# Attention scores in a one-core attention and feed-forward kernel: from stacked operand tiles to pairs of matmuls in the two row halves of TensorE

## The chip, the cores and the metric

One core of one Trainium2 chip runs the whole program. The metric is the device time of one execution in microseconds (us); the median of three executions of the kernel before is 939.8 us. A difference of about 0.2% (some 2 us) is what such a measurement can tell from no change.

## What is computed

Thresholded attention over 8 batches, 8 heads, 576 positions and head dimension 64, then a feed-forward block (FFN) on the result. Everything is float32:

```
scores = scale * q @ k.T
thresh = max(scores, -1) - tau
scores = where(scores >= thresh, scores, -1e9)
attn   = softmax(scores)
x      = attn @ v                        # heads side by side: (8, 576, 512)
xk     = mu_k * x + (1 - mu_k) * x_prev  # x_prev: x one position earlier
xr     = mu_r * x + (1 - mu_r) * x_prev
out    = sigmoid(xr @ w_r) * (relu(xk @ w_k)**2 @ w_v)
```

The weights are 512x1024, 1024x512 and 512x512.

## The kernel before

**Work and order.** The program is recorded first: `add` notes each step with its engine, what it reads and writes, and a planner's cost, and `plan.follow(PLACES)` then puts all steps in the order of a table of numbers (lines 20 to 120). Each engine executes its steps in that order, and so does the one queue that issues DMAs (SP). Nothing is reordered at run time; a step that is not ready holds up what stands behind it on its engine.

**Jobs and units.** Two heads of a batch make a job. A batch has four jobs; in batch 0 each is cut in two halves. A job has units: four of kind P (128 queries of each head against 576 keys) and one of kind T (the last 64 queries of both heads together). There are 128 P units and 32 T units. Per unit: `scores` on TensorE into the PSUM tiles `s` (one per head, two in all); on VectorE the row maximum (line 660); on ScalarE the threshold (668) and the exponential (676); on VectorE the mask with the sum (684), which is the last reader of `s`; then GpSimd's scaling (713).

**Split operands.** The matmul type is fp32r, which keeps fewer bits than float32, so `operands` (479 to 570) splits the scaled q and k of a job into a high part (ScalarE, 521) and the remainder (GpSimd, 531), both in the tile `hl`, and a product is hi·hi + hi·lo + lo·hi. The host lays out q and k "woven": the rows of the two heads alternate. Six DMAs a job (545, 557, 563) pick each head's rows from `hl` and build two stacked tiles: `st1` has q's high and low parts on 128 rows with the high part of k twice; `st2` has the low part of k on the even rows and zeros on the odd ones (set once, 477). Two products of 128 rows then give all three terms. Per P unit and head: two products of two matmuls of 288 columns, four steps a unit at lines 613 to 628, the matmul in line 620.

**Other score paths.** The first four jobs (`plain`) use unsplit float32: a matmul of 64 rows for each head, head 0 in the upper and head 1 in the lower row half of the array (line 602; each matmul is two passes in the trace). The T units take three products of 128 rows straight from `hl` (line 592). Both stay as they are.

**Probabilities to the second product.** In batches 0 and 1 TensorE transposes the probabilities (738) and ScalarE evicts them (754). From batch 2 on a job is "moved": VectorE turns 32x32 blocks into the tile `pt` (774, 787; two units of a group fill one `pt`, of which there is one), a DMA writes it to DRAM (`far`, 798), and a second reads it back into `pm` in the order wanted (803). `attend` (line 930) multiplies by v, 64 columns of the array for each head, side by side.

**FFN.** `ffn_chunk` has the products with w_k (1089), w_r (1131) and w_v (1153), all of 128 rows in fp32r. They stand between the score steps on TensorE once batch 0 has its scores, and alone at the end. `FILL` steps (1245) are transposes of the identity that nothing reads.

Of the kernel before, what the change touches and what calls it, by code (L numbers as in the profile page):

```python
# [8 lines left out]
F32 = mybir.dt.float32  # L9
# [7 lines left out]
KEEP = ('st2', 's', 'w', 'pm', 'pl')  # L17
# [3 lines left out]
FILL = 11  # L21
PLACES = (
    "!$(%*0!%!.!,!0!B!#!!!&!/!)#i!*!f##!>#<#B#e$[!+!H!]!a!u!}#X#h!-!O!`$G$J$k%.%[!2#7#;#c#f$($+$F#O$h(+(5(G(l)I)Q!X#.$I(U",
    "(Z(f):)J#`&V(P)C)G)M)t*,!m#p&%&b&h&q&{)s!A$U)y*)*2*7*?*H#:#v)X)0)o*$*F*O#1$2*9*>*C*G*M*W!S!z*B*N*V*[*c*x!d#H*`*i*p*v",
    "+&+,&B*e*o+%+-+6+y,_#P+]+n,C,D,I,S-z)S+$+F+x+|,$-l/&%O&Z+9+<+N+V+s,1$#,:,s-K-_-e.%.,%I-s/A/7/F/M/R/^#I-=/m/p/s/t/{0;",
    "!(!<#?!1!3!6!7!:!4!9!8!=!@!C!E!D!M!V!I!T!L!W!?!J!P!Q!U!F!K!N!R![!^!b!_!h!q!c!g!l!t#!#%#*#-#6#G!;!s#~!Z!i!o!n!r!e!j!k",
    "!p!y!{!~#4#)#F#W#a#8#E!x#&#,#/#5#+#3#2#9#>#A#D#C#S#g#N#[#R#]#l#s#u#z#|$*!5#@$z#=#J#Q#L#T#K#U#V#Y#_#b#d#{#m$/$,$H$!$4",
    "#^#o#w#x#}#j#t#q#y$%$&$-$)$3$@$7$D$6$A$K$M$O$S$X%z!G!v&?!|#(#M$1#$#n#0#Z$.$$$0$:$9$<$5$=$;$?$C$E$L$P$]$c$g$t$V$^$B$N",
    "$R$T$Y$Q$W$Z$_$e$j$o$r$y%6%!%)$}%3%|&$&)&7&:&C$8$`%L&J(R&*&H&](=(I(_)r*-*8(j(s)L)i)w)z)|*!*6*<*@*D*J+3+Z+d+p+q+u+{,&",
    ",.,/,M,]-u.2.8+>+E+J+P+S+_+b+k,4,i-8-^,{-(-W-b-d-g-w-{.4.U/./3*U*]*b+.+5*Q*Y*h+2+@-X/?/C/L/Q/X070<0O0b1X0J0U0n0r0v11",  # L30
    "151;1B1U#r$>&}$p$w$~%#$u%1%9%D%>$d$i$m$s%$${%(%,%0%8%B%V%M%A%J%P$a$b$v$x$f$l$n$q$|%%%&%*%5%:%?%G%H%R%^%r%T%Y%4%7%+%/",
    "%;%C%F%K%2%<%=%E%W%_%c%g%q&F&,&9%v%x&j&l&r&v&w()(#%-%Z(i%h%u%~&&%t&;&#&+&/%N%Q%S%X%`%b%e%p&3&A&X&z(!&O&`(&%U%]%n%o%a",
    "%d%f%i%s%{%}&(&.&2&5&<&@&M&L&R&S&d%w%y&-&1&!&0&4&=&8&D&>&G&Q&U&i&a(*(4(/(J&|(1(Q(T(W(`(d(r(q&6&^)P&f&x&p(2&n(,(B(<(F",
    "&E&I&K&N&[&W&_&e(Y(^(g)8)3(m).)&&c&g&P&T&k&s&t&y&Y&m&o&u(((-(7(0(?(O(:(@(E(N&~($(3(6(.(>(8(A(;(C(D(L(X(a(k(c(w)+(~)/",
    "(t(x)<)Y)c(9(e+`(o(|)%)((z)>)B)1)7(H(K(M(S(](V(b(h)))9)f)l*#)h)~)x([(p(n(u(v({(})#(y)!)$)*)5)=)E)A)Z)_)N)U)`)j)2)4),",
    ")-)?)O)D)T)6)H)@)K)[)b)}*&*(*5*.*1*;*L*{+0+;/H*r+/,A,J,O,l-I.c/@/j/r/}0]0g0,0^0w1`2P2Z2]2t2y3!3,383=3A3E3]2e2g2x2|3$",
    "3)3M3e3i3q3u3x1~2+20282:2H2M2N2S2W2[2a1y1|2T2V2X2_2d2m3%3+31342232353D3Z3@3Q3U3Y3z464044494B4G4V4d4w5S5Y4-4>4J4R4Z4m",
    "4s4{5!58)F*f-O*t+4+?+D*}+O+U+=+c)R)V)W)])g)d)k*j*n+(+G+f+L+A+R+K)q)u)^)a){*+*%*/)e)m)n)v*4*=*a*A*w*|*I*R*g*k***E*3*:",
    "*S*X*Z*_*K*^*T*d*l*y+W+M+z,!+X+i+^+l,=,n,P*m*s*q*u*~+*+++1*z+!+#+)+r+v,)+},N,V,*,0,W,[+:+B+7+8+H+Q+T+[+C+I+a+g+o+t,,",
    "+w,7,;,3,8,<,Q,a,}+Y,+.s,@-&,H-<,F-J-6-B-F+e+h+j+m+~,(,-,?,B,f,x-E-3,o,z,y,#,%,5,9,2,6,L,R,>,E,G,K,Z,`,u,j-%-.-5-N-$",  # L40
    "-),T,U,X,^,Y,c,d,g,b,e,h,k,q,t,|-1---4-?-S-V-f.6.G.E,r,w,m,p-!-+-,-0,v,~-#-*-:->-C-R-]-i-k-t-q.*-/-2-9-;-7-D-@-G-A-L",
    "-H-Q-Z-`-h-n-|./...L-v.-.W.f-T.@0%.C.R._.{.w/$.[.P.k-M-P-U-Y-a-c-j.#.&.F.T.g.j.M.n.S-[-m-o-r-p-}-y.!-x.$-~.(.5.7.B.>",
    ".h.p.O.a.q.}.).+.1.3.0.;.9.=.:.?.<.A.J.N.o.Z.x/1/;/I/%/+/h0!/y.H.I.D.K.Q.X.Y.^.V.`.].b.i.t.v.|.~/5/0/d/(/9.d.e.m.r.l",
    ".u.z/!.y/)/#/-/>/E/J/O/b/q/T/]/W/Z/u01/*/a2z/g/n0)090P0c0L0T0X/4/6/8/=/N/D/S/Y/o040@0V0H0?0D0A/G/K/,///P/U/V/[/2/:/<",
# [234 lines left out]
def tile_threshold_attention_then_rwkv_ffn(  # L279
# [1039 lines left out]
```

## Time and profile before

| | |
|---|---|
| median of 3 runs | 939.8 us (939.23 to 940.68) |
| profiled execution | 939.09 us, of which the trace spans 937.2 us |
| TensorE matmuls (PE) | busy 902.6 us, 96% of the span, 5881 instructions |
| VectorE (DVE) | 695.9 us, 74% |
| GpSimd (POOL) | 673.0 us, 72% |
| ScalarE (ACT) | 634.7 us, 68% |
| DMA | 226.59 MB, 69.2% of 16 engines' span |
| granted TensorE clock | 0.998 of 2.4 GHz |

Busy time counts a matmul from its start to its modelled end. Matmuls overlap in the pipeline, so the duration of one is more than the distance from its start to the next one's start. PEld is the load of the stationary operand, which runs beside matmuls. A wait is the idle time of an engine just before an instruction, put down to what ended it.

### The profile page before, as it was taken

What the parts mean: (1) busy time and instruction counts of PE and PEld (TensorE: products, weight loads), DVE (VectorE), ACT (ScalarE), POOL (GpSimd) and SP (SyncE); (2) the same over time, 40 slices, a digit from 0 to 9 for tenths busy, and PEclk for the clock granted to TensorE, in tenths of its full rate; (3) what the DMA queues carried; (4) which work ended last, traced back from release to release, by engine and by line L of the source; (5) the groups of instructions that cost most, each with busy time, mean ns of one, the idle gap of its engine ahead of it and who ended that gap; (6) DMA issues with size and microseconds to landing.
All of it is one profiled execution on the core that took longest, in us unless ns stands there. A gap on an engine that the chain in (4) does not pass through costs nothing.

```text
span 937.2 us, 17207 instructions
## 1 busy us (share of the span) xinstructions
PE 902.6 (96%) x5881; PEld 739.3 (79%) x5881; DVE 695.9 (74%) x1503; ACT 634.7 (68%) x1284; POOL 673.0 (72%) x822
## 2 busy tenths in 40 slices
PE   5888999999999999999999999999999999999998
PEld 3465787788888788888887888888888888879986
DVE  4889998898878887888789978788788887810030
ACT  3799999977676767575766575768476766545532
POOL 2688898877778768686787587788678677746531
PEclk9999999999999999999999999999999999999999
DMA  8756333558898988998788878989888887750001
GB/s 316 258 174 203 106 104 115 161 183 305 295 312 307 330 303 316 315 311 301 273 286 299 299 264 314 312 299 315 279 302 313 302 306 266 259 176 23 23 23 23
DMA packets 102327, 226.59 MB, mean 242 GB/s; under 512 B 19296, under 2 KB 32608, under 8 KB 96096
## 3 DMA queue, kind: packets, MB, share of 16 engines
q1 hardware_dynamic: 102240, 225.49, 69.2%
q8 instruction: 47, 0.77, 0.3%
q14 instruction: 40, 0.33, 0.1%
HBM read 108.27 MB, written 73.14 MB: 194 GB/s over the span
## 4 chain that ended last, share of the span: by engine, by line
PE 69%; DVE 10%; ACT 9%; DMA 7%; issue 2%; SPq 1%; POOL 1%; ACTq 0%; DVEq 0%; POOLq 0%
PE w L1153 19%; PE w L1089 16%; PE w L930 12%; PE s L620 10%; PE w L1131 8%; ACT p L676 3%; DVE p L684 3%; DMA st<-hl 2%; DVE pt L774 2%; PE s L592 2%; DMA far<-pt 2%; ACT pm L754 2%; DVE sm L660 2%; PE w L738 1%; PE s L602 1%
## 5 line engine op out<-in xcount | busy, mean ns | idle before, releaser
L684 DVE SCALAR_TENSOR_TENSOR p<-s,sm,p 128x576 f32<-128x576 f32 x288 | 231.8, 811 | 50.8 <-ACT sm L668 24.6
L676 ACT ACTIVATE p<-s,sm 128x576 f32<-128x576 f32 x288 | 209.2, 734 | 84.4 <-DVE sm L660 57.4
L660 DVE TENSOR_REDUCE sm<-s 128x1 f32<-128x576 f32 x288 | 212.9, 750 | 62.1 <-PE s L620 41.6
L713 POOL TENSOR_SCALAR p<-p,sm 128x576 f32<-128x576 f32 x288 | 213.0, 749 | 43.2 <-DVE sm L704 39.8
L1089 PE MATMUL w<-xk,wk 128*128 128x256 f32 x1728 | 229.4, 281 | 0.1
L1153 PE MATMUL w<-wv,k 128*128 128x512 f32 x864 | 220.4, 395 | 0.0
L1089 PEld LDWEIGHTS w<-xk,wk 128*128 128x128 f32 x1728 | 217.0, 188 | 4.1 <-issue 1.6
L1153 PEld LDWEIGHTS w<-wv,k 128*128 128x128 f32 x864 | 156.8, 188 | 30.6 <-issue 1.2
L930 PE MATMUL w<-pm,v 128*64 128x256 f32 (+1 forms) x1280 | 165.4, 410 | 0.8 <-DVE xT L457 0.4
L930 PEld LDWEIGHTS w<-pm,v 128*64 128x64 f32 x1280 | 88.7, 137 | 66.2 <-issue 5.3
L668 ACT ACTIVATE sm<-sm,small 128x1 f32<-128x1 f32 x288 | 81.0, 289 | 68.8 <-DVE sm L660 68.2
L1112 POOL TENSOR_TENSOR k<-r,k 128x512 fp32r<-128x512 f32 x72 | 92.6, 1293 | 48.6 <-ACT k L1102 45.7
L774 DVE STREAM_TRANSPOSE pt<-p 128x1024 f32<-128x1024 f32 x96 | 115.9, 1217 | 5.1 <-DMA end<-pt 1.8
L620 PE MATMUL s<-st 128*128 128x288 f32 x480 | 108.6, 310 | 11.1 <-DVE p L684 10.2
L1131 PE MATMUL w<-wr,xk 128*128 128x512 f32 x432 | 112.6, 395 | 0.0
L531 POOL TENSOR_TENSOR hl<-raw,hl 128x640 fp32r<-128x640 f32 (+1 forms) x64 | 97.9, 1535 | 13.5 <-ACT hl L521 8.2
L696 POOL TENSOR_SCALAR sm<-sm 128x2 f32<-128x2 f32 (+1 forms) x160 | 30.7, 192 | 102.2 <-DVE p L684 84.8
L620 PEld LDWEIGHTS s<-st 128*128 128x128 f32 x480 | 78.7, 188 | 32.0 <-DVE p L684 20.3
L620 PE MATMUL s<-st,st 128*128 128x288 f32 x480 | 101.7, 297 | 0.2 <-DMA st<-hl 0.2
L1131 PEld LDWEIGHTS w<-wr,xk 128*128 128x128 f32 x432 | 77.6, 188 | 15.1 <-issue 0.5
L1097 ACT ACTIVATE r<-w 128x512 f32<-128x512 f32 x72 | 42.4, 594 | 61.5 <-PE w L1089 46.1
L620 PEld LDWEIGHTS s<-st,st 128*128 128x128 f32 x480 | 77.2, 188 | 2.7 <-DMA st<-hl 0.4
(71 smaller groups left out, 1026.3 us busy)
## 6 DMA issues: line engine op xcount, KB each, us to landing
far<-pt SPq DMA_DIRECT2D x48, 1152.0 KB, 5.1
pm<-far SPq DMA_DIRECT2D x48, 1152.0 KB, 6.2
st<-hl SPq DMA_DIRECT2D x64, 288.0 KB, 4.1
raw<-in_qk SPq DMA_DIRECT2D x28, 640.0 KB, 5.0
st<-hl SPq DMA_DIRECT2D x56, 256.0 KB, 3.9
v<-in_v SPq DMA_DIRECT2D x36, 320.0 KB, 3.9
st<-hl SPq DMA_DIRECT2D x64, 144.0 KB, 3.6
out<-sg SPq DMA_DIRECT2D x32, 256.0 KB, 3.8
```

The costliest lines, as they stand in the source:

```text
L531: lambda cs=cs: G.tensor_tensor(hl.get()[:, 1, cs], raw.get()[:, cs], hl.get()[:, 0, cs].bitcast(F32), op=ALU.subtract),
L620: PE.matmul(ss[y].get()[:, z, 0:HS], l.get()[:, c * P : (c + 1) * P], r[:, z * HS : (z + 1) * HS], start=(j == 0), stop=(j == 1),)
L660: lambda sv=sv, col=col: V.tensor_reduce(col(0), sv(), axis=AX.XY, op=ALU.max, negate=True),
L676: lambda sv=sv, pv=pv, col=col: A.activation(pv(), sv(), AF.Exp, bias=col(0)),
L684: lambda sv=sv, pv=pv, col=col: V.scalar_tensor_tensor(pv(), sv(), col(1), pv(), op0=ALU.is_ge, op1=ALU.mult, accum_out=col(2)),
L713: lambda y=y, o=y * S if unit["kind"] == "P" else 0: G.tensor_scalar(p.get()[:, o : o + S], p.get()[:, o : o + S], sm.get()[:, 3, y : y + ...
L774: V.transpose(o, x)
L930: PE.matmul(o[g].get()[hs, 0 : n[g]], vt.get()[:, c, hs], pt, start=(c == 0), stop=(c == 4))
L1089: PE.matmul(h.get()[:, f], l, r, start=(ct == 0 and i == 0), stop=(ct == NCT - 1 and i == 2))
L1112: lambda r=r, js=js: G.tensor_tensor(k2.get()[:, 1, js], r.get().rearrange("p (a b) -> p a b", a=2), k2.get()[:, 0, js].bitcast(F32), op=A ...
L1131: PE.matmul(z.get(), l, r, start=(ct == 0 and i == 0), stop=(ct == NCT - 1 and i == 2))
L1153: PE.matmul(vps.get(), l, r, start=(ft == 0 and i == 0), stop=(ft == NFT - 1 and i == 2))
```

## The change

- `st1`, `st2`, their six DMAs a job, the zeroing and the host's woven layout go. `hl` gets a second buffer.
- A P unit's scores become one step of twelve matmuls: for each of the three products and each half of the keys, head 0 in rows 0 to 63 and head 1 in rows 64 to 127 of the array, straight from `hl`. The step writes both `s` tiles.
- `pt` holds one unit in place of two, with two buffers, and each half goes to DRAM by a DMA of its own.
- The buffers `r` go from two to three, FILL from 11 to 17, and the table of places is a new one.

```diff
-FILL = 11
+FILL = 17
 PLACES = (
...
-    KTURN, KMOVE, RB, DMOVE, TB, FB = 0, 8, 2, 0.35, 1, 8
+    KTURN, KMOVE, RB, DMOVE, TB, FB = 0, 8, 3, 0.35, 2, 8
...
-        hl = job["hl"] = sbuf("hl", [P, 2, WM], FR)
+        hl = job["hl"] = sbuf("hl", [P, 2, WM], FR, 2)
...
-        job["st"] = [(sbuf("st1", [P, SM + S], FR, 3), sbuf("st2", [P, S], FR, 2)) for _ in range(2)]
...
-        for y in range(2):
-            st1, st2 = job["st"][y]
-            for j in range(2):
-
-                def mm(j=j, l=st1, y=y, st1=st1, st2=st2):
                     for z in range(2):
-                        r = st2.get() if j else st1.get()[:, nq - qt : nq - qt + S]
...
-                add("PE", 0.264, mm, reads=[st1, st2] if j else [st1], writes=[ss[y]], key=key + 0.5 * y - 1000, lat=0.44)
...
+        def mm():
+            qs = slice(qt + c * P, qt + (c + 1) * P)
+            for j, (l, r) in enumerate(prods):
+                for z in range(2):
+                    for h in range(2):
+                        hr = slice(h * D, (h + 1) * D)
+                        PE.matmul(
+                            ss[h].get()[:, z, 0:HS],
+                            hl.get()[hr, l, qs],
+                            hl.get()[hr, r, keys(h, z)],
+                            start=(j == 0),
+                            stop=(j == 2),
+                        )
+
+        add("PE", 0.95, mm, reads=[(hl, "hi"), (hl, ("lo", 0)), (hl, ("lo", 1))], writes=list(ss.values()), key=key - 1000, lat=1.15)
...
-                job["turned"][g] = sbuf("pt", [P, NQ, 2, BW], F32, TB)
+                job["turned"][g] = plan.buf(dram, "far", [P, NQ, 2, BW], F32, FB)
+            far, tt = job["turned"][g], sbuf("pt", [P, NQ, BW], F32, TB)
...
+            def away():
+                SY.dma_start(far.get()[:, :, t], tt.get())
+
+            add("DMA", DMOVE, away, reads=[tt], writes=[(far, t)], key=n - KMOVE, kb=576)
```

In the changed file line 577 is the new score matmul, 560 the T units', 883 the product with v, 1042, 1084 and 1106 the FFN's, 617 and 641 the row maximum and the mask, 751 and 757 the two DMAs of a moved group.

**TensorE, around a product with v.** Before (kernel lines as above; x2, x3, x10 count equal instructions in a row):

```order
L1089 MATMUL w_2_145<-xk_1_3105,wk20_0_529 128x256 x3
L620 MATMUL s_0_96<-st1_2_3092 128x288 x2
L1089 MATMUL w_2_145<-xk_1_3105,wk30_0_382 128x256 x3
L1089 MATMUL w_1_138<-xk_1_3105,wk21_0_1062 128x256 x3
L1089 MATMUL w_1_138<-xk_1_3105,wk31_0_788 128x256 x3
L620 MATMUL s_0_96<-st2_0_68,st1_2_3092 128x288 x2
L620 MATMUL s_1_98<-st2_1_70,st1_1_3173 128x288 x2
L1089 MATMUL w_1_138<-xk_1_3105,wk01_0_996 128x256 x3
L930 MATMUL w_0_119<-pm_0_160,v_0_3255 64x320 x10
L930 MATMUL w_2_145<-pm_1_277,v_0_3255 64x256 x10
L620 MATMUL s_0_96<-st1_0_3341 128x288 x2
L592 MATMUL s_1_98<-hl_0_3292 128x288 x6
```

Now (line 577's two rows alternate six times in each of the blocks):

```order
L577 MATMUL s_1_92<-hl_1_3338 128x288
L577 MATMUL s_0_90<-hl_1_3338 128x288
...
L1106 MATMUL w_3_170<-wv30_0_1921,k2_0_3629 128x512 x3
L1106 MATMUL w_2_162<-wv20_0_1544,k2_0_3629 128x512 x3
L1106 MATMUL w_2_162<-wv30_0_1921,k2_0_3629 128x512 x3
...
L577 MATMUL s_1_92<-hl_1_3338 128x288
L577 MATMUL s_0_90<-hl_1_3338 128x288
...
L883 MATMUL w_0_150<-pm_0_160,v_0_3675 64x320 x10
L883 MATMUL w_1_154<-pm_1_249,v_0_3675 64x256 x10
L577 MATMUL s_0_90<-hl_0_3750 128x288
L577 MATMUL s_1_92<-hl_0_3750 128x288
```

Before, score steps of 128 rows stand among FFN steps of 128 rows, two matmuls at a time; now each unit is one block of twelve matmuls of 64 rows, and some blocks stand right beside a product with v. In the whole order the array goes 99 times from one of its divisions (full, row halves, column halves) to another before, and 297 times now. There are 120 blocks at line 577; of their 240 edges 46 are shared with a product with v.

**VectorE, two P units in a row** (`sm` and `p` are of the unit, `s_0` and `s_1` of the head). Before:

```order
L684 SCALAR_TENSOR_TENSOR p_2_4794,sm_2_4770<-s_1_98,sm_2_4770,p_2_4794 128x576
L660 TENSOR_REDUCE sm_2_4770<-s_0_96 128x1
L660 TENSOR_REDUCE sm_1_4721<-s_1_98 128x1
L684 SCALAR_TENSOR_TENSOR p_2_4794,sm_2_4770<-s_0_96,sm_2_4770,p_2_4794 128x576
L704 RECIPROCAL sm_0_4711<-sm_0_4711 128x1
L684 SCALAR_TENSOR_TENSOR p_0_4729,sm_1_4721<-s_1_98,sm_1_4721,p_0_4729 128x576
```

Now:

```order
L617 TENSOR_REDUCE sm_1_4546<-s_1_92 128x1
L744 STREAM_TRANSPOSE pt_0_4553<-p_2_4443 128x4x32
L617 TENSOR_REDUCE sm_1_4546<-s_0_90 128x1
L641 SCALAR_TENSOR_TENSOR p_1_4559,sm_1_4546<-s_1_92,sm_1_4546,p_1_4559 128x576
L731 STREAM_TRANSPOSE pt_1_4573<-p_0_4512 128x2x4x128
```

Before, the next unit's first maximum could stand ahead of this unit's last mask; that is so between P units in 8 of 95 places, and in none now, since the block needs both `s` tiles free.

**SP, one job's DMAs.** Before:

```order
L545 DMA st1_1_3631<-hl_0_3621 128x1x512
L563 DMA st2_1_70<-hl_0_3621 64x576
L545 DMA st1_2_3748<-hl_0_3621 128x1x512
L557 DMA st1_2_3748<-hl_0_3621 128x1x576
L563 DMA st2_0_68<-hl_0_3621 64x576
L492 DMA raw_0_3782<-in_qk 128x1280
```

Now:

```order
L479 DMA raw_0_4480<-in_qk 128x1280
L751 DMA far_6_4504<-pt_0_4463 512x1x288
L751 DMA far_6_4504<-pt_1_4509 512x1x288
```

The 192 DMAs into `st1` and `st2` are gone, and 96 writes to `far` stand where 48 stood; the queue issues 470 DMAs in place of 614.

## Rows read from the trace of the kernel before

**Rows 1.** The page, part 1: busy time and share of the span.

```profile
PE 902.6 (96%) x5881; PEld 739.3 (79%) x5881; DVE 695.9 (74%) x1503; ACT 634.7 (68%) x1284; POOL 673.0 (72%) x822
```

**Rows 2.** Windows (from:to, length, busy of each engine with its count).

```profile
core 0: us, PE busy (x) PEld busy (x) DVE busy (x) ACT busy (x) POOL busy (x), PEclk, DMA share, GB/s
20.00:120.00 100.00, 87.69 (x572) 61.58 (x570) 88.39 (x192) 89.16 (x200) 81.82 (x107) 0.98 0.54 187
200.00:800.00 600.00, 595.46 (x3924) 495.77 (x3923) 494.64 (x1054) 399.12 (x787) 450.37 (x546) 1.00 0.86 299
```

**Rows 3.** The page, part 4: the chain that ended last, by engine.

```profile
PE 69%; DVE 10%; ACT 9%; DMA 7%; issue 2%; SPq 1%; POOL 1%; ACTq 0%; DVEq 0%; POOLq 0%
```

**Rows 4.** Waits of PE: for what, total us, times, longest.

```profile
PE s L620 <- DVE p L684: 10.2, 15, 1.8
PE s L602 <- ACT raw L500: 7.1, 1, 7.1
...
PE w L1245 <- ACT pm L754: 3.0, 3, 1.8
PE s L592 <- DVE p L684: 1.3, 1, 1.3
...
PE s L620 <- DMA st<-hl: 0.4, 2, 0.2
```

**Rows 5.** Timeline of PE near 403 us: start, length, instructions and their count.

```profile
403.30 0.43 PE L620 MATMUL s<-st,st 128*128 128x288 f32 x2
403.56 0.42 PE L620 MATMUL s<-st 128*128 128x288 f32 x2
403.83 0.43 PE L620 MATMUL s<-st,st 128*128 128x288 f32 x2
404.09 3.36 PE L1089 MATMUL w<-xk,wk 128*128 128x256 f32 x27
```

**Rows 6.** Lines by form: count, busy us, mean ns of one.

```profile
L620 PE MATMUL s<-st,st 128*128 128x288 f32 x480 | 101.7, 297 | 0.2 <-DMA st<-hl 0.2
L1153 PE MATMUL w<-wv,k 128*128 128x512 f32 x864 | 220.4, 395 | 0.0
L1089 PE MATMUL w<-xk,wk 128*128 128x256 f32 x1728 | 229.4, 281 | 0.1
L684 DVE SCALAR_TENSOR_TENSOR p<-s,sm,p 128x576 f32<-128x576 f32 x288 | 231.8, 811 | 50.8 <-ACT sm L668 24.6 <-ACT p L676 24.1 <-PE w L738 0.2
```

**Rows 7.** Line 602, row halves: duration ns min/median/max of each kind.

```profile
L602 PEld LDWEIGHTS s<-xk x32: 182/186/187, 31.5 to 47.0; 64*128 64x128 f32 x32
L602 PE MATMUL s<-xk x32: 402/403/507, 31.5 to 47.3; 64*128 64x288 f32 x32
```

**Rows 8.** Timeline of PE, 30.5 to 33.2 us: one P unit of line 602.

```profile
31.28 0.33 PE L738 MATMUL w<-ident,p 128*128 128x128 f32 x1
31.54 1.24 PE L602 MATMUL s<-xk 64*128 64x288 f32 x8
32.97 0.44 PE L738 MATMUL w<-ident,p 128*128 128x128 f32 x2 [0.19 <-POOL p L713]
```

**Rows 9.** Timeline of PEld, 31.53 to 31.66 us: the loads under way then.

```profile
31.54 0.30 PEld L602 LDWEIGHTS s<-xk 64*128 64x128 f32 x4
```

**Rows 10.** Timeline of PE, 386 to 395 us: a product with v between matmuls of 128 rows.

```profile
385.66 1.32 PE L1153 MATMUL w<-wv,k 128*128 128x512 f32 x5
386.91 5.07 PE L930 MATMUL w<-pm,v 128*64 128x320 f32 x40
391.91 0.52 PE L620 MATMUL s<-st 128*128 128x288 f32 x2
392.27 0.42 PE L620 MATMUL s<-st,st 128*128 128x288 f32 x2
```

**Rows 11.** Line 620's records up to 120 us (columns as in rows 2, PE and PEld alone).

```profile
0.00:120.00 120.00, 18.30 (x94) 13.58 (x94) 0.99 0.58 207
```

**Rows 12.** The chain in order of time: DMAs into the stacked tiles before 100 us.

```profile
69.71 3.77 DMA st<-hl
...
82.45 5.23 DMA st<-hl
```

**Rows 13.** DMA issues: count, KB each, median us to landing.

```profile
far<-pt SPq DMA_DIRECT2D x48, 1152.0 KB, 5.1
...
st<-hl SPq DMA_DIRECT2D x64, 288.0 KB, 4.1
```

More of the change, by code (lines that the diff above doesn't have):

```diff
@@ L578, in keys @@
         def keys(y, z):
-            k0 = nq - qt + (ST if unit["kind"] == "P" and y == 0 else 0)
+            k0 = nq + (ST if unit["kind"] == "T" or y == 0 else 0)
             return slice(k0 + z * HS, k0 + (z + 1) * HS)
-        if unit["kind"] == "T" and not job["plain"]:
-            hl = job["hl"]
-            prods = [(0, 0), (0, 1), (1, 0)]
-            for j, (v_, r) in enumerate(prods):
-                def mm(j=j, v_=v_, r=r):
-                    k = hl.get()[:, r, nq : nq + S + ST]
-                    for z in range(2):
-                        x = k[:, ST + z * HS : ST + (z + 1) * HS]
-                        PE.matmul(ss[1].get()[:, z, 0:HS], hl.get()[:, v_, 0:P], x, start=(j == 0), stop=(j == 2))
-                add("PE", 0.264, mm, reads=[(hl, ("lo", 0) if v_ else "hi"), (hl, ("lo", 1) if r else "hi")], writes=[ss[1]], key=key - 1000, lat=0.47)
-            return
         if job["plain"]:
@@ L612, in scores, with mm @@
             return
-        for y in range(2):
-            st1, st2 = job["st"][y]
-            for j in range(2):
-                def mm(j=j, l=st1, y=y, st1=st1, st2=st2):
+        hl = job["hl"]
+        prods = [(0, 0), (0, 1), (1, 0)]
+        if unit["kind"] == "T":
+            for j, (l, r) in enumerate(prods):
+                def mm(j=j, l=l, r=r):
                     for z in range(2):
-                        r = st2.get() if j else st1.get()[:, nq - qt : nq - qt + S]
                         PE.matmul(
-                            ss[y].get()[:, z, 0:HS],
-                            l.get()[:, c * P : (c + 1) * P],
-                            r[:, z * HS : (z + 1) * HS],
+                            ss[1].get()[:, z, 0:HS],
+                            hl.get()[:, l, 0:P],
+                            hl.get()[:, r, keys(1, z)],
                             start=(j == 0),
-                            stop=(j == 1),
+                            stop=(j == 2),
                         )
-                add("PE", 0.264, mm, reads=[st1, st2] if j else [st1], writes=[ss[y]], key=key + 0.5 * y - 1000, lat=0.44)
+                add("PE", 0.264, mm, reads=[(hl, ("lo", 0) if l else "hi"), (hl, ("lo", 1) if r else "hi")], writes=[ss[1]], key=key - 1000, lat=0.47)
+            return
+        def mm():
+            qs = slice(qt + c * P, qt + (c + 1) * P)
+            for j, (l, r) in enumerate(prods):
+                for z in range(2):
[6 more added lines that the diff above has]
+                            start=(j == 0),
+                            stop=(j == 2),
+                        )
+        add("PE", 0.95, mm, reads=[(hl, "hi"), (hl, ("lo", 0)), (hl, ("lo", 1))], writes=list(ss.values()), key=key - 1000, lat=1.15)
     def softmax(unit):
@@ L806, in back @@
                     )
-                add("DMA", DMOVE, away, reads=[tt], writes=[far], key=n - KMOVE, kb=1152)
                 add("DMA", DQ, back, reads=[far], writes=[(pm, "moved")], key=n - KMOVE, kb=1152)
```

244 lines of the change are left out of this document (95 added, 149 removed).

## The prediction

> **What bounds the kernel.** I read the busy times first, then the same by window, then the chain of waits and the waits themselves. TensorE is busy 96% of the span, VectorE 74% [rows 1]. By window there are two regimes [rows 2]: from 200 to 800 us TensorE is busy 595.5 of 600 us, VectorE 494.6; from 20 to 120 us TensorE is busy 87.7 of 100 us, with VectorE and ScalarE at 88 and 89. TensorE is 69% of the chain that ended last [rows 3]. It waited 11.5 us for masks to free the `s` tiles (10.2 + 1.3) and 0.4 us for the stacked tiles' DMAs [rows 4]. So after about 120 us a microsecond of TensorE's own time is a microsecond of the result, and the DMAs that go are hidden almost wholly. The question is what the scores cost TensorE in either form.
>
> **What goes.** 120 P units times 8 matmuls at line 620. Their distance from start to start is the cost, not their duration: six take 403.30 to 404.09, 0.132 us each [rows 5]. 960 x 0.132 = 126.7 us. A duration minus that distance, 297 - 132, is about 163 ns of pipeline that overlaps with the next one. By the same subtraction a matmul of line 1153 costs 395 - 163 = 232 ns [rows 6].
>
> **What comes.** 120 blocks of 12 matmuls of 64 rows. Whether two of them run side by side is read from line 602, which has this form in plain float32. Eight of its passes take 1.24 us [rows 8]. One lasts 402 ns, and 507 at most [rows 7]: the first ones carry 0.105 us in which they wait for their own weights. 1.24 - 0.163 - 0.105 = 0.97 us for eight passes, each of which streams 402 - 163 = 240 ns. One after the other they would need 1.9 us, so they go in four pairs, 0.243 us a pair. The weight loads go side by side too: four loads of 186 ns are done within 0.30 us [rows 7, 9]. So a block has six slots.
>
> A slot in fp32r is not in the trace. A float32 pass streams 288 columns in 240 ns, an fp32r matmul in 132. Bounds: 0.1215 us, half of line 602's pair, and 0.264, two matmuls of line 620 one after the other. I take 0.132, the nearest row: the same type and columns, and a pair reads the same 128 rows. 720 x 0.132 = 95.0 us (87.5 at the lower bound). The slots save 31.7 us.
>
> **What a change of the array's division costs.** Every block is cut off from its neighbours, which use 128 rows. The trace shows this price at the product with v [rows 10]. In front: five matmuls of 0.232 us should take 1.16 us from 385.66, but the product begins after 1.25, so 0.09 us are lost. Then comes the load that nothing hides, 0.105 us for 128 columns [rows 7] (half of that for the product's 64). Into a block: 0.195 us. Line 602 agrees: the transposition ahead of it starts at 31.28 and the first pass 0.26 us later, where two transpositions are 0.11 apart (0.44 - 0.33) and 0.05 is its own load [rows 8]. Behind: the product's 40 passes are ten pairs of 320 and ten of 256 columns; at 0.243 us per 288 columns they need 4.85 us, 0.05 more for the first load, and took 5.00 (386.91 to 391.91), so 0.10 us are lost. The next two matmuls then need 0.36 us in place of 0.264: 0.095 for the first load. Out of a block: 0.195 us, if row halves leave as column halves do.
>
> A block by itself costs 6 x 0.132 + 0.39 = 1.18 us, where the eight matmuls cost 1.06. Of the 240 edges 46 are shared with a product with v, which pays such edges already; a shared one saves one way out and one way in less what the common edge costs, about 0.195 us. In all 120 x 0.39 - 46 x 0.195 = 37.8 us. TensorE has 37.8 - 31.7 = 6.1 us more to do. Line 620 has 94 records before 120 us, 12 units [rows 11]; there TensorE has idle time [rows 2], and their part, 12 x 0.12 = 1.5 us, costs nothing. That leaves +4.6 us.
>
> The Trainium skill (TensorEngine Tiling (Array Packing), Key Properties) says that changing the tiling mode drains TensorE. The trace agrees: it is the 0.09 to 0.10 us above. The same page (Theoretical Speedup) promises up to 2x where the contraction has at most 64 rows and gives the change of mode no price; by that alone the sum would be -31.7 us, and the rows on the product with v speak against it.
>
> **Waits.** The twelve matmuls write both `s` tiles, so a block stands until this unit's second mask is done, where a head's own step needed its own mask alone. Behind it on TensorE stand FFN matmuls that were ready; VectorE's next maximum waits for the block. Where TensorE already waits (15 and 1 times [rows 4]), the wait can grow by a mask, 0.81 us [rows 6], some 13 us in all. That is the upper bound. Below: these 11.5 us can vanish, because TensorE, with more to do, comes later to each block; and two DMAs into stacked tiles on the early chain, 3.8 and 5.2 us [rows 12], go with the tiles. Between -20 and +13 I take 0: VectorE keeps a sixth of its time free, and the order of before already lets the next unit's first maximum pass the last mask in only 8 of 95 places.
>
> **The rest at nothing.** 192 DMAs fewer into the stacked tiles and 48 more, smaller ones to `far` [rows 13]: TensorE waited 0.4 us for the first kind; the half that is late (the second) is now half as large, and SP has fewer issues in front of every later one. If that cover failed, `pm` would be late and `attend` would stand. Six FILL steps are 18 transposes in the first units, where TensorE waits on ScalarE anyway [rows 4]; if not, 18 x 0.11 = 2 us [rows 8]. Two memsets of VectorE, ahead of the first scores, go. The third `r` buffer frees ScalarE earlier, which is not the bound.
>
> **Sum.** The profiled execution took 939.1 us (the median is 939.8). 939.1 + 4.6 = 943.7; I say 944 us, slower by half a per cent.
>
> **Rivals.**
> 1. *Cheap slots (faster).* A pair that costs half of line 602's, 0.1215 us, takes off 720 x 0.0105 = 7.6 us: 936. It turns the forecast to faster below 0.124 us a slot (720 x 0.0083 = 6 us). Waits for masks that vanish beside it would lead down to 928. For: line 602's pairs take 0.243 us where each pass streams 0.240, so pairing itself costs next to nothing. Against: every fp32r matmul of the trace needs more than half of what a float32 pass of its columns needs, 132 against 120 ns here, and a pair feeds as many rows.
> 2. *The joint wait (clearly slower).* Every block that is tied to the second mask makes a wait grow: 943.7 + 13 = 957. For: the block has no slack of half a unit. Against: see above.
> 3. *The halves don't run side by side in fp32r.* If a load of 0.105 us and a stream of 0.132 follow each other in each half, a slot takes 0.237: 720 x 0.105 = +76, 1020 us; with matmuls one after the other 0.264, 1039. Against: line 602, loads and all. The Trainium skill (TensorE: Matmul & The Clock Gate, Part 3) has a load overlap with running matmuls only where the row group differs, which would give this rival; the trace differs, since line 620 loads all 128 rows beside every matmul at 0.132 us.
> 4. *Edges without a price.* If the way in and out hid behind queued work, TensorE would have 31.7 us less: 907 us. Against: the product with v pays at both ends.
>
> **Chances.** The sum, 944 (its own range 939 to 952): 0.48, of which 0.34 slower by over 0.2% and 0.14 within it. Rival 1: 0.30 (0.27 faster, 0.03 the same). Rival 2: 0.12. Rival 3: 0.04. Rival 4: 0.06. So faster by over 0.2% (about what a measurement of this kernel can tell from no change) 0.33, the same 0.17, slower 0.50. The range for 8 in 10 is 928 to 960: it takes in rivals 1 and 2 and leaves out 3 and 4 and a little of each of the others.
>
> **What would show it.** At line 577 two matmuls start together and twelve take 0.8 us from the first to the last pair, at 0.132 a pair. TensorE loses 0.09 us in front of each block and 0.10 behind it, and the first matmuls on either side last 0.1 us longer than the others. FFN distances stay at 0.118 and 0.232. Waits of line 577 for the mask (641) stay near 11 us; at 25, rival 2 is right. Wrong is the whole if block and edges together take under 1.0 us (faster) or over 1.4.

## The result and the profile after

The changed kernel takes 947.97 us (five executions, 946.17 to 951.89), the kernel before beside it 939.8. The ratio is 1.0090, 95% interval 1.0062 to 1.0118. A second set (e14, six executions) gave 948.98 us and 1.0093 [1.0063, 1.0123]. So it is slower by 0.9%, some 8.5 us; the forecast was 944 us, 928 to 960. The profiled execution took 947.9 us.

The page, part 1, and the chain that ended last, by engine (before: [rows 1, 3]):

```profile
PE 910.9 (96%) x6379; PEld 716.1 (76%) x6379; DVE 697.8 (74%) x1501; ACT 631.2 (67%) x1284; POOL 672.3 (71%) x822
...
PE 86%; DVE 6%; ACT 4%; issue 1%; DMA 1%; POOL 1%; SPq 0%; ACTq 0%; DVEq 0%; POOLq 0%
```

Windows, as in [rows 2]:

```profile
core 0: us, PE busy (x) PEld busy (x) DVE busy (x) ACT busy (x) POOL busy (x), PEclk, DMA share, GB/s
20.00:120.00 100.00, 88.89 (x636) 61.82 (x635) 83.71 (x182) 85.77 (x196) 77.45 (x104) 0.98 0.38 130
200.00:800.00 600.00, 599.53 (x4308) 474.00 (x4305) 498.90 (x1062) 400.65 (x798) 454.06 (x551) 1.00 0.74 246
```

TensorE leaves 0.5 of 600 us unused, where it left 4.5. The DMA share of the middle falls from 0.86 to 0.74, and the DMAs drop out of the chain (1% where they were 7%). The stacked tiles were really a load; it was one that TensorE hardly felt.

A block of twelve matmuls between FFN matmuls, in the timeline of PE (compare [rows 5]):

```profile
403.39 2.99 PE L1042 MATMUL w<-xk,wk 128*128 128x256 f32 x24
406.31 1.06 PE L577 MATMUL s<-hl 64*128 64x288 f32 x12
407.31 3.97 PE L1042 MATMUL w<-xk,wk 128*128 128x256 f32 x31
```

The starts of the single matmuls in this stretch (the same trace, one by one): last FFN matmul 406.106; first pair at 406.315 and .318, the next ones at 406.552, .686, .815, .947 and 407.080; next FFN matmuls 407.305, 407.526, 407.646. Normal distances are 0.118 for the FFN and 0.132 for a pair. So 0.209 - 0.118 = 0.09 us are lost in front; the second pair comes 0.237 after the first, 0.105 too late; the pairs are 0.13 apart; 0.225 - 0.132 = 0.09 us are lost behind; and the second FFN matmul comes 0.221 after the first, 0.10 too late. Block and edges together are 1.185 us in the median of the blocks that stand among FFN matmuls.

Lines by form (compare [rows 6]):

```profile
L1042 PE MATMUL w<-xk,wk 128*128 128x256 f32 x1728 | 223.7, 284 | 0.0
L1106 PE MATMUL w<-wv,k 128*128 128x512 f32 x864 | 215.2, 399 | 0.0
L577 PE MATMUL s<-hl 64*128 64x288 f32 x1440 | 133.6, 310 | 8.5 <-DVE p L641 8.2
```

The FFN's matmuls last 3 to 4 ns longer in the mean (281 and 395 before), which is about what 0.1 us at each edge makes, spread over all of them. Waits of PE (compare [rows 4]):

```profile
PE s L577 <- DVE p L641: 8.2, 14, 1.4
PE s L542 <- DVE p L641: 7.6, 4, 2.7
PE s L542 <- ACT raw L487: 6.9, 1, 6.9
```

The blocks wait 8.2 us for masks, where line 620 waited 10.2. The `s` tiles as a whole cost as much as before: with the T units (0.5 now, 1.3 before) and the unsplit jobs (line 542, 7.6 now; before, the row below, which [rows 4] does not have) 16.3 us now and 15.6 before.

```profile
PE s L602 <- DVE p L684: 4.1, 3, 2.7
```

The waits for stacked tiles are gone.

What the joint step does shows at 158.7 us (timeline of PE, idle time before in brackets):

```profile
158.72 0.39 PE L577 MATMUL s<-hl 64*128 64x288 f32 x1 [0.76 <-DVE p L641]
159.53 1.06 PE L577 MATMUL s<-hl 64*128 64x288 f32 x11 [0.41 <-DVE p L641]
```

One matmul starts when the first head's mask is done, and the other eleven stand 0.81 us for the second head's mask, because the heads alternate in the block. Eight of the first 24 blocks (those of batches 0 and 1, up to about 195 us) show such a gap, 0.44 to 1.47 us; of the 96 later ones three, 0.46 to 0.62 us, between 518 and 537 us.

Last, the granted clock. TensorE ran at 0.5 of it (1.2 GHz) in two stretches of some 3.4 us, which the kernel before does not have there. The first, beside the same time in e13 (an experiment below that differs in the form of the first 24 blocks), by windows of PE:

```profile
core 0: us, PE busy (x), PEclk, DMA share, GB/s
92.00:94.00 2.00, 0.58 (x5) 1.00 0.04 15
94.00:96.00 2.00, 1.57 (x14) 1.00 0.00 0
96.00:98.00 2.00, 2.00 (x10) 0.56 0.00 0
98.00:100.00 2.00, 2.00 (x12) 0.59 0.00 0
```

and in e13:

```profile
92.00:94.00 2.00, 0.62 (x6) 1.00 0.03 8
94.00:96.00 2.00, 1.84 (x13) 1.00 0.00 0
96.00:98.00 2.00, 2.00 (x18) 1.00 0.00 0
98.00:100.00 2.00, 1.97 (x16) 1.00 0.27 64
```

Both waited some 1.4 us for a mask; only the changed kernel falls to half clock behind it. The block in the changed kernel also stands a second time (timeline of PE, the changed kernel's two rows and then e13's):

```profile
94.01 0.40 PE L577 MATMUL s<-hl 64*128 64x288 f32 x1 [1.43 <-DVE p L641]
94.83 1.06 PE L577 MATMUL s<-hl 64*128 64x288 f32 x11 [0.42 <-DVE p L641]
...
93.72 1.60 PE L592 MATMUL s<-hl 128*128 128x288 f32 x9 [1.38 <-DVE p L690]
```

The changed kernel's product with v then hands over late, and VectorE stands (timeline of DVE in the changed kernel):

```profile
98.65 0.08 DVE L641 DVE_READ_ACCUMULATOR p<-s,sm,p 128x1 f32 x1
100.46 0.22 DVE L713 COPY xE<-w 128x64 f32<-128x64 f32 x1 [1.73 <-PE w L883]
```

while in e13 the copy comes 0.05 us after the mask:

```profile
98.31 0.08 DVE L690 DVE_READ_ACCUMULATOR p<-s,sm,p 128x1 f32 x1
98.44 0.22 DVE L762 COPY xE<-w 128x64 f32<-128x64 f32 x1
```

### The profile page after: what moved, and what is told of

Same layout as the page of the kernel before. It is cut to its first block, busy times and chain, and to the rows that moved or that the text cites. A ratio compares the mean times of both kernels' runs of the same rounds, so it can differ in the third digit from the quotient of the medians.

```text
span 946.1 us, 17817 instructions
## 1 busy us (share of the span) xinstructions
PE 910.9 (96%) x6379; PEld 716.1 (76%) x6379; DVE 697.8 (74%) x1501; ACT 631.2 (67%) x1284; POOL 672.3 (71%) x822
## 4 chain that ended last, share of the span: by engine, by line
PE 86%; DVE 6%; ACT 4%; issue 1%; DMA 1%; POOL 1%; SPq 0%; ACTq 0%; DVEq 0%; POOLq 0%
PE w L1106 21%; PE w L1042 21%; PE w L883 16%; PE s L577 12%; PE w L1084 10%; PE s L560 3%; PE w L695 2%; DVE p L641 2%; ACT p L633 2%; DVE sm L617 2%; PE s L542 1%; DVE r L999 1%; ACT pm L711 1%; ACT sm L625 0%; DVE m L999 0%
## 5 line engine op out<-in xcount | busy, mean ns | idle before, releaser
L617 DVE TENSOR_REDUCE sm<-s 128x1 f32<-128x576 f32 x288 | 208.4, 748 | 76.3 <-PE s L577 57.5
L1042 PE MATMUL w<-xk,wk 128*128 128x256 f32 x1728 | 223.7, 284 | 0.0
L1042 PEld LDWEIGHTS w<-xk,wk 128*128 128x128 f32 x1728 | 213.4, 189 | 8.9 <-issue 5.1
L1106 PE MATMUL w<-wv,k 128*128 128x512 f32 x864 | 215.2, 399 | 0.0
L1106 PEld LDWEIGHTS w<-wv,k 128*128 128x128 f32 x864 | 159.3, 188 | 39.9 <-issue 5.5
L577 PE MATMUL s<-hl 64*128 64x288 f32 x1440 | 133.6, 310 | 8.5 <-DVE p L641 8.2
L577 PEld LDWEIGHTS s<-hl 64*128 64x128 f32 x1440 | 102.7, 184 | 43.6 <-DVE p L641 24.7
L1112 DVE TENSOR_TENSOR sg<-w,sg 128x512 f32<-128x512 f32 x36 | 24.4, 681 | 67.4 <-PE w L1106 56.0
L711 ACT ACTIVATE pm<-w 128x512 f32<-128x512 f32 (+3 forms) x128 | 52.7, 446 | 11.0 <-PE w L695 10.3
```

The lines of the kernel that those rows point to most:

```text
L577: PE.matmul(ss[h].get()[:, z, 0:HS], hl.get()[hr, l, qs], hl.get()[hr, r, keys(h, z)], start=(j == 0), stop=(j == 2),)
L617: lambda sv=sv, col=col: V.tensor_reduce(col(0), sv(), axis=AX.XY, op=ALU.max, negate=True),
L1042: PE.matmul(h.get()[:, f], l, r, start=(ct == 0 and i == 0), stop=(ct == NCT - 1 and i == 2))
L1106: PE.matmul(vps.get(), l, r, start=(ft == 0 and i == 0), stop=(ft == NFT - 1 and i == 2))
```

## The experiments

Each kernel has one profile; its times and its mean clock are of all its executions. "Progress" below is the end of the k-th row maximum of the program: a lag that appears between two of them belongs to that stretch. The kernel before was run beside each group: 939.3 us (e1 to e4), 940.4 (e5, e6, e7, e11), 938.9 (e8, e12, e13), 940.2 (e14), so kernels of different groups are compared by their ratios, and 0.001 of a ratio is 0.94 us.

| run | us | ratio to before | mean clock |
|---|---|---|---|
| changed, 11 executions | 948.5 | 1.0090, 1.0093 | 0.9933 |
| e1 half tiles only | 942.63 | 1.0041 [1.0026, 1.0056] | 0.9972 |
| e2 no FILL | 951.84 | 1.0142 [1.0119, 1.0165] | 0.9878 |
| e3 full rows, joint | 938.92 | 1.0004 [0.9991, 1.0017] | 0.9972 |
| e4 full rows, split | 936.8 | 0.9981 [0.9965, 0.9996] | 0.9976 |
| e5 early full, split | 943.19 | 1.0027 [1.0014, 1.0041] | 0.9978 |
| e6 late full, split | 941.97 | 1.0031 [1.0013, 1.0049] | 0.9940 |
| e7 early, one head at a time | 949.35 | 1.0093 [1.0073, 1.0112] | 0.9942 |
| e8 early full, joint | 943.85 | 1.0051 [1.0031, 1.0070] | 0.9980 |
| e11 fills ahead of blocks | 953.07 | 1.0128 [1.0105, 1.0150] | 0.9930 |
| e12 fills in unused columns | 949.3 | 1.0100 [1.0079, 1.0122] | 0.9955 |
| e13 as e8, nine matmuls | 944.75 | 1.0065 [1.0047, 1.0082] | 0.9992 |

**e1, the half tiles alone.** The kernel before, with `pt` in two halves and two DMAs a group:

```diff
-    tt = sbuf("pt", [P, NQ, 2, BW], F32, 1)      # one DMA of 1152 KB a group
+    tt = sbuf("pt", [P, NQ, BW], F32, 2)         # two DMAs of 576 KB
```

> The kernel before, with one part of the change alone: the turned probabilities in two half tiles with two buffers, each half written to DRAM by its own DMA; the first half's DMA stands in the queue right behind the later of its two transpositions, the rest of the order is that of before. If the scores are the cause of the 8 us, this stays at 940 us, or gains up to 3 us where VectorE had waited for the one tile. If the half tiles (twice the writes, in smaller pieces) are the cause, it goes to 944 or more.

Slower by 0.4%, between the two times of the expectation. The waits of PE name most of it, 2.6 of 3.9 us (in [rows 4] the row on `st` has 0.4 us):

```profile
PE s L635 <- DVE p L699: 10.0, 15, 1.8
...
PE s L635 <- DMA st<-hl: 3.0, 3, 1.4
```

In the old order the added DMAs delay the DMAs into the stacked tiles. The changed kernel has none of those, so this price is not part of its result; there `far<-pt` lands in 3.8 us (5.1 before) and no wait of TensorE names it.

**e2, without FILL.**

```diff
-    lambda pt=pt: [PE.transpose(...) for c in range(3)],
+    lambda: None,
```

> The changed kernel with all 17 FILL steps empty (51 transpositions that nothing reads). If they stand where TensorE waits anyway, the time stays at 948 us within 1.5; if they take time from the early chain, it falls by up to 51 x 0.11 = 5.6 us, to 942; if they keep the clock up, it rises by 2 us or more and the granted clock of the first 100 us falls.

Taking all 17 FILL steps away makes the changed kernel 0.5% slower, with the lowest clock of all runs. They are not at nothing: they keep the clock up, as the third case of the expectation has it (the first 100 us of the profile have a mean granted clock of 0.95, and 0.98 with the steps). What the six added ones alone are worth was not run.

**e3 and e4, full rows from `hl`.** The new order with everything else, but eight matmuls of 128 rows in place of twelve of 64, four for one head and then four for the other: e3 in one step, always head 0 first, e4 in two steps, first the head whose maximum VectorE takes first.

```diff
-    for j, (l, r) in enumerate(prods): for z in range(2): for h in range(2):
-        PE.matmul(ss[h]..., hl[hr, l, qs], hl[hr, r, keys(h, z)], ...)
+    for h in range(2): for j in range(2): for z in range(2):      # e4: a step for each h
+        PE.matmul(ss[h]..., hl[:, 0, qs], hl[:, j, keys(h, z)], ...)
```

> The changed kernel with each block of twelve matmuls of 64 rows replaced by eight of all 128 rows straight from the split tile, still one step that writes both score tiles. It sums both heads in one score and leaves out the third product, so its scores are other numbers; what follows is the same work. No edges and no row halves are left, the joint wait and the new order are. If TensorE's own time is the cause (edges 38 us, slots saved 32), 942 us. If the joint wait in batches 0 and 1 is the cause, the blocks' length matters little there and 942 to 946 us. If the new order or the half tiles are, 946 us or more.

> As the run with eight matmuls of 128 rows in one step (same change to the computation), but in two steps of four, one for each head, right behind each other on TensorE; the head whose maximum stands first on VectorE goes first, and each step waits for its own head's mask alone. Against that run this takes away the joint wait and nothing else. If the joint wait costs the 9 us that the trace shows before 200 us, it gains 5 to 9 us on that run (933 to 938); if not, it is within 2 us of it.

e3 came out below all three of its cases, and e4's gain just above the 2 us of its second. e3 is as fast as the kernel before: the row-half form costs some 8 us (0.0088 of 940; 1.0092 stands for the changed kernel's two sets from here on), and all the rest of the change together nothing.

e4 is 0.0023 lower, 2.2 us, but not for the reason in the expectation. In e3 too each head's four matmuls wait for their own mask alone: near 94 us the first head's start at 94.22 and the second head's 0.81 later, and in e4 at 92.38 and 0.81 later. What differs is the hand-over. Where VectorE takes head 1's maximum first, it waits for all eight matmuls in e3 and for the first four in e4: in eight of the first 24 blocks a waiting maximum starts 0.04 us behind the block's end in e3 and 0.25 to 0.49 us ahead of it in e4. So 2.2 us is, as the traces have it, the price of this joint hand-over. What it costs that eleven matmuls of the changed kernel, and not four, stand for the second mask is part of the row-half form here; no run takes it away alone.

By progress (73rd maximum at 197.2, 194.0 and 192.0 us in the changed kernel, e3 and e4; 145th at 399.5, 394.2 and 391.7; 288th at 820.1, 810.5 and 808.4) the hand-over's price is all there by the 73rd, and the row halves' price has an early part, 3.2 us, and one that grows evenly after it.

**e5 and e6, one part of the program each.** e4's scores in batches 0 and 1 alone (e5), or in the others alone (e6).

```diff
+    if job["b"] < 2:        # e6: if not job["b"] < 2
+        (the two full-row steps of e4)
+        return
```

> The changed kernel, but in the first two batches (24 blocks, up to about 195 us) the scores are eight matmuls of 128 rows straight from the hl tile, as two steps of four, one a head, each behind its own mask. These scores are other numbers (both heads are mixed and the third product is left out); the 96 late blocks stay row halves. Theory A (a block is 0.128 us longer than eight full matmuls; in the first 200 us, where block, maximum and mask follow each other, that counts in full; late, less what shared edges give back, 6.1 us; the joint wait is worth 2.0 us and all of it early): 948.0 - 24 x 0.13 - 2.0 = 943 us, 942 to 944. Rival B (the whole price sits in the first 200 us: the wait for the second mask and the two more stretches of half clock at 96 and 175 us, and the late blocks cost nothing): 948.0 - 8.9 - 2.0 = 937. Rival C (early blocks cost nothing because TensorE idles there, as the prediction had it): 946 to 948.

> The mirror image: row halves in the first two batches, eight matmuls of 128 rows in two steps, one a head, in the 96 late blocks (those scores are other numbers and leave the third product out). Theory A: 948.0 - 96 x 0.128 + 32 shared edges x 0.195 = 948.0 - 6.1 = 942 us, 941 to 943; splitting brings nothing here, because no late block of the changed kernel has a gap between its first and second pair. Rival B: 947 to 948. With e5 the two gains should add up to the 11.2 us between the changed kernel and e4.

The times are those of theory A in both: 943.2 and 942.0 us. B and C fall. (That no late block has a gap is not quite so: three have, above.) For the late blocks its sum holds: they cost 1.0092 - 1.0031 = 0.0061, 5.7 us. The early ones with the hand-over cost 0.0065, 6.1 us; theory A has 5.1 and puts all of the 3.1 beside the hand-over down to the block's length, which e13 below does not bear out. The two add up to 0.0126, e4's distance is 0.0111; the intervals cover that.

**e7, one head at a time in the early part.** Six matmuls for one head behind its own mask, then six for the other.

```diff
+    if job["b"] < 2:
+        a = first()                       # the head whose maximum comes first
+        add("PE", ..., lambda: alone(a), writes=[ss[a]])
+        add("PE", ..., lambda: alone(1 - a), writes=[ss[1 - a]])
+        return
```

> The changed kernel with the scores of the first two batches as two steps, one a head: six matmuls of 64 rows for one head as soon as its own mask is done, then six for the other, so that no wait is joint but no two matmuls run side by side. The product is the reference's. If each needs a slot of 0.132 us, the two steps take 12 x 0.132 + 0.39 = 1.97 us in place of 1.18. If the joint wait is what costs early (10 blocks of the changed kernel stand 5.8 us in all between their first and second matmul for a second mask): 946, 2 us faster. If a block's length counts in full early: 948 + 24 x 0.79 - 2 = 965. I expect 955 to 965. And if a 64-row load doesn't hide behind a matmul in the same row half, the distance is 0.237 us and the time above 975.

I expected 955 to 965; it is as fast as the changed kernel. (The ten blocks of the expectation are nine, one of them with 0.31 us, and it is 7.0 us from their first matmuls' starts to the second's.) The premise that no two matmuls run side by side holds only where the second mask is late, as at the block that stood at 158.72 above:

```profile
158.60 1.87 PE L605 MATMUL s<-hl 64*128 64x288 f32 x12 [0.59 <-DVE p L693]
160.40 1.83 PE L935 MATMUL w<-pm,v 128*64 128x320 f32 x12
```

The twelve need 1.80 us to the next matmul, and so does the paired block of the changed kernel there (1.80 at 158.72): the first six run in the time in which that block stands for the second mask. Where both masks are done, in 16 of the 24 blocks, the second head's matmuls run beside the first head's after all:

```profile
58.14 1.44 PE L605 MATMUL s<-hl 64*128 64x288 f32 x12
59.51 1.08 PE L935 MATMUL w<-pm,v 128*64 128x256 f32 x8
```

Here the second head's first matmul, the seventh of the order, starts 0.38 us after the first head's first and ahead of its fourth, and the twelve need 1.37 us; the paired block needs 0.99 to 1.29. All 24 blocks together hold TensorE 4.5 us longer than the changed kernel's, not 24 x 0.79 = 19. So e7 sets 4.5 us of TensorE's time against an earlier hand-over of the first head's scores, and its time tells the price of neither alone. It also shows that a load hides behind a matmul in the same row half: unpaired matmuls start 0.129 to 0.134 us apart, from the second on.

**e11 and e12, fills ahead of the blocks that wait.** Transposes of the identity, in e11 into `w` tiles, in e12 into columns 384 to 511 of the block before's score tiles.

```diff
+    for k in [5, 7, 15, 17, 20]:          # e12: (7, 10), (15, 6), (17, 6), (20, 8)
+        (right ahead of block k: six transposes into a w tile; e12: so many into the s tile of block k - 1)
```

> The changed kernel with six transposes of the identity (0.66 us of TensorE) put right ahead of the blocks 5, 7, 15, 17 and 20, which wait 0.13, 1.43, 0.76, 0.76 and 1.03 us for their first mask in the changed kernel's profile. If the two stretches of half clock behind such waits (96 and 175 us) cost time: they go, and the time falls by 1 to 3 us, to 945 to 947. If they cost nothing because VectorE is the bound there: 948 +- 0.5; with what the fills delay (0.53 us ahead of block 5) at most 949.

> As e11, but the transposes of the identity write into unused columns of the score tiles of the block before, so that they wait for no eviction of a w tile: 10, 6, 6 and 8 of them ahead of the blocks 7, 15, 17 and 20, no more than fits into the wait for the first mask there. If the stretches of half clock behind such waits cost time: they go and the time falls to 945 to 947. If VectorE is the bound there all the same: 948 +- 0.7.

e11 did not test what it was to test: its fills stand 7.3 us for a `w` tile that ScalarE has to evict, and hold the blocks up; both stretches of half clock are still there. The fills of e12 don't run in the wait for the first mask either, since their tile is one that this mask reads. They stand for it themselves and hold the block up behind it:

```profile
97.46 1.31 PE L1233 MATMUL s<-ident 128*128 128x128 f32 x10 [1.44 <-DVE p L661]
98.70 1.06 PE L594 MATMUL s<-hl 64*128 64x288 f32 x12
```

Both stretches of half clock are gone even so, behind the same wait, and the time stayed. Its windows of PE show why the time of this execution does not tell what they cost:

```profile
70.00:72.00 2.00, 1.14 (x6) 0.79 0.42 135
72.00:74.00 2.00, 2.00 (x15) 0.50 0.31 127
74.00:76.00 2.00, 2.00 (x10) 0.50 0.03 8
76.00:78.00 2.00, 2.00 (x11) 0.51 0.00 0
...
96.00:98.00 2.00, 0.56 (x6) 1.00 0.00 0
98.00:100.00 2.00, 2.00 (x22) 1.00 0.00 0
```

The half clock came earlier instead, at 37 and at 71 to 78 us, behind other waits, and for longer. Its two executions with a clock of 0.999 took 946.2 us, the four at 0.993 to 0.995 took 949.2 to 950.2.

**e8 and e13, the length of an early block alone.** e3's joint form in batches 0 and 1, and the same with a ninth matmul for head 0, which was to make a block as long as one of row halves.

```diff
-    for j, z in [(0, 0), (0, 1), (1, 0), (1, 1)]:
+    for j, z in [(0, 0), (0, 1), (1, 0), (1, 0), (1, 1)]:      # head 0 alone
```

> The changed kernel, but the first two batches (24 blocks) score with eight matmuls of 128 rows from the hl tile in one step behind both masks, as the changed kernel's block does; those scores are other numbers (both heads mixed, the third product left out). It differs from the changed kernel early by the block's form alone: 948.0 - 3.1 = 945 us by e3 against the trace of the changed kernel. It is the base for e13.

> As e8 (the first 24 blocks in 128-row form behind both masks, scores other numbers), with a ninth matmul in each of these blocks, so that a block lasts 1.19 us, as a row-half block does, in full-row form. If the early price is the block's length (the next maximum starts 0.13 us later): as the changed kernel, 948, and no stretch of half clock at 96 and 175 us is needed for it. If the early price comes with those stretches, which the profiles show with row halves (changed kernel, e6, e7) and not without (e3, e4): as e8, 945, or at most 1 us more.

e8 came as expected (1.0051 is 944.6 us beside 939.8), and e13 at the edge of its second case. The ninth matmul costs 0.0014, 1.3 us by the ratios and 0.9 by the medians of the same chip; the executions with a clock of 0.999 or 1.000 stand at 943.1 and 944.7 us. The early row halves cost 1.0092 - 1.0051 = 0.0041, 3.9 us. What is left, 2.5 us, has two candidates.

The first is length that e13 does not have. Where the second mask comes late (seven of the 24 blocks), e13 has five matmuls done before it, the ninth among them, and its last four take 0.79 us from the first start to the end; the changed kernel's eleven take 1.06. By these numbers that is 7 x 0.27 = 1.9 us at most, an estimate.

The second is the half clock. In the traces (changed kernel against e13) the lag is 0.3 us up to the 36th maximum, with two of those seven blocks already past, jumps by 1.7 us at the 37th, at 103 us, behind the first stretch of half clock, and is 2.8 us at the 73rd, after a step of 0.7 at the 66th (179 us), behind the second one. e12 settles what the first jump is: it has row halves and full clock there, and its copy follows the mask as e13's does (timeline of DVE):

```profile
102.54 0.09 DVE L661 DVE_READ_ACCUMULATOR p<-s,sm,p 128x1 f32 x1
102.66 0.22 DVE L733 COPY xE<-w 128x64 f32<-128x64 f32 x1
```

Its 37th maximum comes 4.0 us behind the 36th, as in e13 (4.0); in the changed kernel 5.7. So these 1.7 us are the price of the half clock and not of the form. At a clock of 0.999 the two executions of e12 still need 946.2 us, where e13 needs 944.7 on the same chip: 1.5 us for what the fills delay and for length together.

**e14, the changed kernel again.**

> The changed kernel once more, for its granted clock. Over all executions so far the time falls by about 0.5 us for each 0.001 of mean granted clock, whatever the kernel; the changed kernel's five executions had 0.988 to 0.998, mean 0.994, where the kernel before had 0.997 and e8 and e13 0.998 and 0.999. If the row halves of the first 200 us bring stretches of half clock with them (theory): the mean is again 0.993 to 0.995 and the time 947 to 949, and the profile shows such stretches behind the waits near 96 and 175 us. If the low mean came from one odd execution: 0.997 and 946.5 to 947.

As the theory had it: 948.98 us, clocks 0.990 to 0.995, mean 0.993. The two stretches are back, a little later:

```profile
98.00:100.00 2.00, 2.00 (x10) 0.52 0.00 0
100.00:102.00 2.00, 2.00 (x11) 0.63 0.00 0
...
176.00:178.00 2.00, 1.46 (x10) 0.65 0.00 0
178.00:180.00 2.00, 2.00 (x10) 0.50 0.00 0
```

and so is the step from the 36th to the 37th maximum, 5.7 us. This profile has two stretches more, near 38 and 72 us. The "whatever the kernel" of the expectation is not so: in the 74 executions of the kernel before beside e1 to e14, the time falls by 0.1 us for 0.001 of clock, and by 0.15 in e1.

No version that beats both came out of this. e4's time cannot be had as it stands, since its scores are not the ones wanted; stacked tiles in the new order, with its two `hl` and three `r` buffers, were not tried.

## Why the prediction was right, and where its terms were off

**Slots: right.** Two matmuls of 64 rows start 3 to 4 ns apart, and a pair takes 0.132 us, as a matmul of 128 rows does. Rival 1 (0.1215) and rival 3 (0.237) fall; for the loads e7 says the same without pairs. (297 - 132 is 165 and not 163; the 2 ns change nothing.) The rule of the Trainium skill that stood behind rival 3 (TensorE: Matmul & The Clock Gate, Part 3) does not hold in these rows.

**Edges: right.** 0.09 and 0.105 into a block, 0.09 and 0.10 out of it; 1.185 us measured, 1.18 forecast. The edges of line 602 and of the product with v [rows 7, 8, 10] had the price in another form of the same thing, and rival 4 falls. Late, where TensorE is the bound, the forecast's own terms give 96 x 0.128 less the edges shared there, 6.1 us; e6 measured 5.7.

**The early part: wrong in the reason.** "Their part, 12 x 0.12 = 1.5 us, costs nothing", because TensorE has idle time there. It has, but the early row halves (the 24 blocks up to 195 us; the forecast's 12 are those up to 120) cost 3.9 us. The idle time is time in which VectorE waits for scores: in the first 200 us its maxima wait 8.4 us for the blocks of the changed kernel, 6.7 for e13's and 5.2 for e8's. A block that is longer delays the next maximum (0.9 to 1.5 us over 24 blocks, e13), and the low clock behind the waits delays everything TensorE hands over (1.7 us at one place, e12). How the rest splits between the two stays open. The clock was in no term of the sum. That the half clock near 96 and 175 us goes with the row halves is shown by the runs: such stretches stand in the profiles of the changed kernel, e6, e7, e11 and e14 (and e2), none at these places in e3, e4, e5, e8 and e13. The mean clocks agree: 0.993 to 0.994 (e2 0.988) against 0.997 to 0.999. It is not the form alone, since e12 has row halves and full clock there. And stretches at other places come in both forms: at 36 to 40 us, ahead of the first block, in e3, e8, e12 and e14, and at 49 to 53 us in e5.

**Waits: the balance right by luck, its parts not.** Forecast 0 between -20 and +13. The 11.5 us of waits that it started from left out 4.1 us of line 602; with them the waits of TensorE for masks are 15.6 us before and 16.3 after. The joint hand-over costs 2.2 us (e3 against e4, e5 against e8 alike), all of it in the first 200 us, and it was in no term; rival 2's mechanism, the wait for the second mask, is in the trace (eight early blocks, three late ones), but what it costs was not measured apart from the form. Against that, the rest of the change earns about 1.8 us: e4, which has all of it and neither the joint hand-over nor row halves, is at 0.9981. That the two nearly cancel was not foreseen. How the gain splits between the stacked tiles' DMAs, the order and the third `r` buffer was not taken apart.

**At nothing.** The half tiles and their DMAs: no wait of the changed kernel names them. FILL: wrong in kind, since the 17 steps as a whole are worth some 0.5%.

**Sum.** Late 5.7, early 3.9, hand-over 2.2, the rest -1.8: 10.0 us by differences of ratios whose intervals are 0.001 to 0.003 wide to either side, against 8.5 measured. The forecast had +6.1, nearly all of it late, and -1.5. Its sign and the larger term were right; the mis-sized one is the early part, -1.5 where it was +3.9 of itself.

## What to carry to other kernels

Two row halves side by side take the slots down (here from eight to six, 0.26 us), and the change of the array's division takes 0.09 us and a bare load of 0.10 us each way; with 0.39 us of edges a block must save three slots of 0.132 us before it gains, or share its edges with work in the same division. Where an engine has idle time because others wait for it, do not book its extra work at nothing: ask when the result is handed over and what the granted clock does behind the wait. A step that writes two tiles in turn waits for the readers of both and hands both over at its end; look in the timeline for a first instruction that stands alone, 0.8 us ahead of the others. And before a run is read as its plan says, look in its trace whether the plan came true: e3, e7, e12 and e13 each did something else than intended.

## What the runs showed of the hardware

- The mean granted clock goes with the time from execution to execution: the changed kernel took 946.17 us at 0.998, 948.5 at 0.993 and 951.89 at 0.988. A straight line with one slope for all twelve kernels beside the one before gives 0.56 us for each 0.001 of clock; the kernel before has 0.1 and e1 0.15.
- After the same wait of 1.4 us TensorE falls to half clock (0.5, which is 1.2 GHz) in one form of the scores and stays at full clock (2.4 GHz) in the other (windows of the changed kernel and e13). With ten transposes between the wait and the block of row halves it stays at full clock too (e12).
- Matmuls of 64 rows that follow each other in the same row half start 0.13 us apart, loads included (e7). Going over to the other half, the first one starts 0.05 us after the last, and the next 0.237 us later (read in the block at 94 us).
- The two row halves don't wait for each other's turn: with six matmuls of one half ahead of six of the other in the order, the second half's first matmul starts 0.38 us after the first one of all and ahead of the first half's fourth (e7, block at 58 us).
